# A spectral filter ahead of a GELU block: first and forward stage on sums and differences, forward stage in bursts of 64x64 tiles

## The chip, the cores and the metric

The kernel runs on one core of a Trainium2 chip. The metric is the device time of one launch in microseconds. Five engines work beside one another on that core: TensorE (PE in the profile, its weight loads PEld), VectorE (DVE), ScalarE (ACT), GpSimd (POOL) and SyncE (SP). POOL and SP issue most of the DMAs here.

## The reference

```python
X = np.fft.rfft(x, axis=1)                      # x: 8 x 3008 x 256
Y = X * (filt_r + 1j * filt_i)[None]            # 1505 frequencies x 256 channels
y = np.fft.irfft(Y, n=3008, axis=1)             # 8 x 3008 x 256
h = y.reshape(24064, 256) @ w_in                # 256 x 2048
g = 0.5 * h * (1 + erf(h / sqrt(2)))            # exact GELU
out = g @ w_out                                 # 2048 x 256, float32
```

## The kernel before

The transform of 3008 = 47 x 64 points is split: n = 64 n1 + n2, and k = k1 + 47 j. All arithmetic on TensorE takes bf16 or fp16 operands.

- **s1** is the first stage. It contracts over n1 (47) for each n2 and gives 24 values of k1 with a real and an imaginary part (48 rows). Each call of `s1(b, c)` does 16 of the 64 values of n2 in eight matmuls of 47x64 tiles with 512 columns, two tiles in the rows of the array by two in its columns. Four PSUM banks are evacuated (L306 on VectorE, L304 on ScalarE) and stored to R1 in DRAM by SP. `r1` reads R1 back with n2 and the real or imaginary part on the partitions.
- **s2** is the forward stage. For each k1 it contracts over n2 and re/im (128 rows) to 64 complex outputs (128 columns). One call `s2(b, p)` does two k1: two 128x128 matmuls of 256 columns (L427), and at once one VectorE product (L430) with the filter F, once for its real and once for its imaginary part.
- **s3** is the backward stage, four k1 pairs per call, sixteen 64x64 tiles with 512 columns (L444). Two `s3_out` evacuate to v_sb, stored to R2. `r2` reads it back as d_sb.
- **s4** finishes the inverse transform (L473) into the ring y_sb, 512 tokens of which form a token tile.
- **mm1** (L592) is y @ w_in for 128 hidden columns, followed by a GELU on ScalarE (L595). **mm2_seven** (L665) is g @ w_out in the seven products of Strassen's scheme: sums_1 (L634), sums_2 (L640) and sums_3 (L647) on VectorE make its operands, and VectorE adds its products (L680 to L694) from two PSUM banks ps_o into the output tiles ost, which POOL stores.

The order of all engines' work is written out by a list of slots. A token tile is 16 slots. A slot has one mm1 and seven matmuls of mm2_seven for the tile before (in the first 16 slots, mm1 alone). What else belongs to a slot is put into `at` by the function names, and issued ahead of the slot's mm2_seven and mm1. For each batch b from 1, `hi` is the slot at which its first token tile is due; s1, r1, s2 and s3 have fixed distances from it, s4 is placed backwards from its due slot into slots that are not in `busy`, and in `crowd` its evacuation goes to ScalarE. Batch 0 is transformed ahead of slot 0 by other functions (c1, c1t, c2, c3, c3t, c4), with its own tables.

PSUM has three banks "h" (mm1; also one bank of each s1 and s3), two "o" (ps_o) and three "f" (s1, s2, s3, s4). [...] `load_next` loads a part of the next batch of x from POOL, behind a `gate`: a one-element copy on POOL that waits for a product of s2. `load_filters_again` rewrites F from batch 0's layout to the one of the others.

Of the kernel before, what the change touches and what calls it, by code (L numbers as in the profile page):

```python
# [19 lines left out]
K1 = 24  # L20
# [11 lines left out]
class _Mix:  # L32
    def __init__(self, ctx, tc, x, filt_r, filt_i, w_in, w_out, out):
# [12 lines left out]
        self.pp = pool("pp", 6)  # L46
# [11 lines left out]
        self.T2p = c.tile([128, K1, 2, 2, 2, 16], BF16, name="T2p")  # L58
# [20 lines left out]
    def load_x(self, b, lo=0, n=32, hs=(0, 1)):  # L79
        nc = self.nc  # L80
        if lo == 0 and 0 in hs:
            self.st[b, "x"] = self.px.tile([128 if b else 2 * NA, HB, 256], BF16, tag="x", name="x_sb")
        xt, o = self.st[b, "x"], 64 if b else NA
        xv = self.x[b].rearrange("(n1 h w) d -> h n1 w d", h=2, w=HB)
        for w in range(lo, lo + n, 8):
            for h in hs:
                nc.gpsimd.dma_start(out=xt[h * o:h * o + NA, w:w + 8, :], in_=xv[h][:, w:w + 8, :])  # L87

# [20 lines left out]
    def load_filters_again(self, eng, k0, k):  # L109

        for o in range(0, 128, 32):
            i = self.st["Fd"][o // 64, :, :, :, k0:k0 + k, :].rearrange("q i t k c -> (q i) t (k c)")
            eng.dma_start(out=self.F[o:o + 32, :, k0:k0 + k, :], in_=i)
# [11 lines left out]
    def load_next(self, b, p, c, h):  # L125

        if b > 0:
            self.gate(self.st[b, "p", p][0:1, 0, 0:1])
        self.load_x(b + 1, 8 * c, 8, (h,))
# [41 lines left out]
    def table_2_rows(self, g):  # L171


        v = self.nc.vector
        ts = v.tensor_scalar
        col = lambda name, dt=FP32: g.tile([128, 1], dt, name=name)
        ri_i, h_i, w_i = col("ri_i", I32), col("h_i", I32), col("w_i", I32)
        ts(out=h_i, in0=self.pi, scalar1=1, scalar2=1, op0=ALU.logical_shift_right, op1=ALU.bitwise_and)
        ts(out=w_i, in0=self.pi, scalar1=2, scalar2=None, op0=ALU.logical_shift_right)
        ts(out=ri_i, in0=self.pi, scalar1=1, scalar2=None, op0=ALU.bitwise_and)  # L180
        self.n2, self.ri = col("n2"), col("ri")
        v.scalar_tensor_tensor(out=self.n2, in0=h_i, scalar=float(HB), in1=w_i, op0=ALU.mult, op1=ALU.add)
        ts(out=self.n2, in0=self.n2, scalar1=1.0 / self.S, scalar2=None, op0=ALU.mult)
        ts(out=self.ri, in0=ri_i, scalar1=-0.25, scalar2=TURNS + 0.25, op0=ALU.mult, op1=ALU.add)
# [40 lines left out]
    def weights_4(self, g):  # L225

        ts = self.nc.gpsimd.tensor_scalar
        h, q, self.wt, self.wts = (g.tile([128, 1], FP32, name=n) for n in ("h48", "q48", "wt", "wts"))
        ts(out=h, in0=self.p, scalar1=48.0, scalar2=None, op0=ALU.is_ge)
        ts(out=q, in0=h, scalar1=-48.0, scalar2=-1.0, op0=ALU.mult, op1=ALU.add)  # L230
        self.nc.gpsimd.tensor_tensor(out=q, in0=self.p, in1=q, op=ALU.add)
        self.nc.gpsimd.tensor_tensor(out=q, in0=q, in1=q, op=ALU.mult)
        ts(out=q, in0=q, scalar1=1.0, scalar2=-1.0, op0=ALU.is_equal, op1=ALU.mult)
# [43 lines left out]
    def table_3_copy(self, q, turn):  # L277

        k = slice(8 * q, 8 * q + 8)
        if turn < 2:  # L280
            self._evac(self.T3[:, k], self.t3.rearrange("p (k w e) -> p k e w", k=8, e=4), "act")
        if turn:
            v = self.t3.rearrange("p (k w h r) -> p k h r w", k=8, h=2, r=2)
            for r in range(2):
                self._evac(self.T3i[:, k, r::2, :], v[:, :, :, 1 - r, :], "act", self.turn[r])

    def table_3_turn(self, q):

        k = slice(8 * q, 8 * q + 8)
        for r in range(2):  # L290
            self.nc.vector.tensor_scalar(out=self.T3i[:, k, r::2, :], in0=self.T3[:, k, 1 - r::2, :],
# [27 lines left out]
    def table_2_parities(self):  # L319
        t = self.T2.rearrange("p k r (s j e) -> p k r s j e", s=2, e=2)  # L320
        for par in range(2):
            for q in range(2):
                self.nc.gpsimd.tensor_copy(out=self.T2p[:, :, par, :, q, :], in_=t[:, :, :, q, :, par ^ q])

    def table_u_rows(self, g):
# [3 lines left out]
        v.tensor_copy(out=self.u0[:, 0], in_=self.T3[:, 0, 0:2, :])  # L329
        v.tensor_copy(out=self.u0[:, 1], in_=self.T3i[:, 0, 0:2, :])  # L330
# [14 lines left out]
    def table_4_rows(self, g):  # L345
# [5 lines left out]
        for x in range(2):  # L351
            for r in range(2):
                t = self.T1[0:NA, 24 * (x ^ r):24 * (x ^ r) + 24].rearrange("p (a k) -> p a k", k=2)
                v.tensor_copy(out=self.T1g[:, x, r], in_=t.unsqueeze(2).to_broadcast([NA, 12, 2, 2]))
        t = self.T2.rearrange("p (a k) r j -> p r a j k", k=2)[:, 0, :, 0:2, :]
        for r in range(2):
            v.tensor_copy(out=self.T2g[:, r], in_=t)

    def table_4_factors(self, g):
# [7 lines left out]
        self.fcs = t[:, 96:224].rearrange("p (w h r) -> p w h r", h=2, r=2)  # L367
# [16 lines left out]
    def s1(self, b, c):  # L384
# [4 lines left out]
        if b == 1 and c == 3:  # L389
            a = [self.pp.tile([128, 2, 512], BF16, tag="p12", name="p12") for i in range(2)]  # L390
        else:
            at = self.pa.tile([128, 4, 512], BF16, tag="a", name="a_sb")
            a = [at[:, 0:2], at[:, 2:4]]
        x = self.st[b, "x"]
        ps = [[self.bank("ps_s1", "h" if i == h == 0 else "f") for h in range(2)] for i in range(2)]
        for i in range(2):
            for r in range(2):
                for h in range(2):
                    w = 8 * c + 4 * r + 2 * i
                    nc.tensor.matmul(ps[i][h][64 * r:64 * r + 64, :], lhsT=self.T1s[64 * h:64 * h + NA],  # L400
                                     rhs=x[64 * h:64 * h + NA, w:w + 2, :], start=True, stop=True)
        for i in range(2):
            for h in range(2):
                self._evac(a[i][:, :, 256 * h:256 * h + 256], ps[i][h].rearrange("p (w c) -> p w c", w=2),
                           "act" if h and (b > 1 or i) else False)
        o = self.st[b, "R1"].rearrange("(w h) q c -> q w h c", h=2)
        for r in range(2):
            w, q = 8 * c + 4 * r, slice(64 * r, 64 * r + 48)
            if b == 1 and c == 3:
                for i in range(2):  # L410
                    nc.sync.dma_start(out=o[:, w + 2 * i:w + 2 * i + 2], in_=a[i][q].rearrange("q w (h c) -> q w h c", h=2))
            else:
                nc.sync.dma_start(out=o[:, w:w + 4], in_=at[q].rearrange("q w (h c) -> q w h c", h=2))
# [8 lines left out]
    def s2(self, b, p):  # L422
        nc = self.nc
        ps = self.bank("ps_s2")
        for i in range(2):
            k = 2 * p + i
            nc.tensor.matmul(ps[:, 256 * i:256 * i + 256], lhsT=self.T2p[:, k].rearrange("p a b c d -> p (a b c d)"),  # L427
                             rhs=self.st[b, "b", k // 6][:, k % 6, :], start=True, stop=True)
        w = self.st[b, "p", p] = self.pp.tile([128, 2, 512], BF16, tag="p12", name="p12")
        nc.vector.tensor_tensor(out=w, in0=ps.unsqueeze(1).to_broadcast([128, 2, 512]),  # L430
                                in1=self.F[:, :, 2 * p:2 * p + 2, :].rearrange("p t a b -> p t (a b)"), op=ALU.mult)
# [18 lines left out]
    def s3_out(self, b, u, i):  # L450
        ps = self.st[b, "ps3"][i]
        vt = self.pv.tile([128, 4, 256], BF16, tag="v", name="v_sb")
        for par in range(2):
            self._evac(vt[:, 2 * par:2 * par + 2, :].rearrange("p a b -> p (a b)"), ps[par],
                       "act" if par or b < 3 else False)
# [30 lines left out]
    def c1(self, grp, half, eng):  # L486

        if grp == 0 and half == 0:
            n = 4 * K1 * 2 * HB
            self.at = self.y0[:, 4608:4608 + n].rearrange("c (a k n h r) -> c a k n h r", a=2, k=K1, h=2, r=2)  # L490
        ps = self.bank("ps_c1", "n")
        x = self.st[0, "x"]
        for i in range(4):
            self.nc.tensor.matmul(ps[:, 96 * i:96 * i + 96], lhsT=x[:, 4 * grp + i, 128 * half:128 * half + 128],
                                  rhs=self.T1c, start=True, stop=True)
        self._evac(self.at[:, half].rearrange("c k n h r -> c k n (h r)")[:, :, 4 * grp:4 * grp + 4, :],
                   ps[:, 0:384].rearrange("c (i k e) -> c k i e", i=4, e=4), eng)

    def c1t(self, q, eng):
# [3 lines left out]
        for i in range(8):  # L503
            self.nc.tensor.transpose(ps[:, 128 * i:128 * i + 128],
                                     self.at[:, i % 2, 4 * q + i // 2].rearrange("c n h r -> c (n h r)"), self.eye)
# [4 lines left out]
    def c2(self, p):  # L510

        nc = self.nc
        w = self.st[0, "p", p] = self.pp.tile([128, 2, 512], BF16, tag="p12", name="p12")
# [220 lines left out]
def kernel(  # L734
# [20 lines left out]
    m.load_x(0, 0, 8)  # L755
    m.k48 = m.iota(g, "k48", [128, 2, K1], [[0, 2], [1, K1]])
    m.load_x(0, 8, 8, (0,))
# [5 lines left out]
    m.load_x(0, 8, 8, (1,))  # L763
    cols = m.cols = m.iota(g, "cols", [128, 128], [[1, 128]])
    m.load_x(0, 16, 16)
# [11 lines left out]
    t3 = m.pg.tile([128, 2, K1, 4, HB], BF16, tag="g", name="T3")  # L777
# [10 lines left out]
    for u in range(16):  # L788
        m.c1(u // 2, u % 2, False if u in (1, 3, 5, 7, 8, 10, 12, 14) else act)
        if u == 3:  # L790
# [4 lines left out]
            nc.vector.tensor_copy(out=m.T1q, in_=m.T1.rearrange("p (h r k) -> p k h r", h=2, r=2))  # L795
# [47 lines left out]
    m.load_x(1)  # L843
# [23 lines left out]
    for b in range(1, B):  # L867
        hi = first(b)
        if b == 1:
            s1, n1, r1, s2, n2, group = 0, 3, 12, 28, 3, 14  # L870
        elif b == 2:
            s1, n1, r1, s2, n2, group = hi - 87, 3.7, hi - 73, hi - 64, 3.4, 14
        else:
            s1, n1, r1, s2, n2, group = hi - 94, 3.7, hi - 80, hi - 70, 3.4, 14
        unit = lambda p: s2 + group * (p // 4) + int(n2 * (p % 4))
        busy.update(range(s1 - 1, s1 + int(3 * n1) + 2))
        for c in range(4):
            put(s1 + int(c * n1), m.s1, b, c)
            put(r1 if c < 3 else unit(3) + 1, m.r1, b, c)
        for p in range(12):  # L880
            put(unit(p), m.s2, b, p)
            busy.add(unit(p))
            if p % 4 == 3:
                put(unit(p) + 3, m.s3, b, p // 4)
                put(unit(p) + 4, m.s3_out, b, p // 4, 1)
                busy.update(range(unit(p) + 2, unit(p) + 6))
        after[b] = unit(11) + 7
        crowd.update(range(s2, after[b]))
        if b + 1 < B:
            for i in range(8):  # L890
                put(unit(i + 2), m.load_next, b, i + 2, i // 2, i % 2)

    for b in range(1, B):
# [8 lines left out]
        for u in range(7, -1, -1):  # L902
            due = (b * S + GRP * u) // TCH * 16
            end = min(end, due - 2 + 6 * (u == 0 and b == 1))
            for half in (1, 0):
                while end in busy:
                    end -= 1
                assert end > after[b] + 8
                put(end, m.s4, b, u, half, act if half or end in crowd or b == 1 and u == 0 else False)
                busy.add(end)  # L910
                end -= 2
# [7 lines left out]
    put(3, m.table_4_factors, g)  # L919
    put(4, m.table_u)  # L920
# [58 lines left out]
```

## Time and profile before

| | |
|---|---|
| median of 3 runs | 746.34 us (745.94 to 746.36) |
| the profiled execution, its span | 747.16 us, 745.3 us |
| TensorE busy, matmuls | 728.5 us (98%), 8287 |
| VectorE busy, instructions | 573.2 us (77%), 1028 |
| ScalarE busy, instructions | 557.5 us (75%), 1000 |
| POOL busy, instructions | 227.7 us (31%), 424 |
| L430 products | 84 of 1220 ns |
| L427 forward matmuls | 168 |
| DMAs of x on POOL | 64 of 188 KB, 4.1 us to landing |

Busy time counts an instruction from its start to its end, and neighbours overlap: two matmuls of 512 columns start 0.22 us apart, though a record lasts 0.38 us. What an instruction costs its engine is the distance between starts, which the timeline view gives. A line with a count of xN is a run of N instructions of one kind.

### The profile page before, as it was taken

What the parts mean: (1) busy time and instruction counts of PE and PEld (TensorE: products, weight loads), DVE (VectorE), ACT (ScalarE), POOL (GpSimd) and SP (SyncE); (2) the same over time, 40 slices, a digit from 0 to 9 for tenths busy, and PEclk for the clock granted to TensorE, in tenths of its full rate; (3) what the DMA queues carried; (4) which work ended last, traced back from release to release, by engine and by line L of the source; (5) the groups of instructions that cost most, each with busy time, mean ns of one, the idle gap of its engine ahead of it and who ended that gap; (6) DMA issues with size and microseconds to landing.
All of it is one profiled execution on the core that took longest, in us unless ns stands there. A gap on an engine that the chain in (4) does not pass through costs nothing.

```text
span 745.3 us, 20244 instructions
## 1 busy us (share of the span) xinstructions
PE 728.5 (98%) x8287; PEld 518.7 (70%) x8420; DVE 573.2 (77%) x1028; ACT 557.5 (75%) x1000; POOL 227.7 (31%) x424
## 2 busy tenths in 40 slices
PE   7999999999999999999999999999999999999998
PEld 4856675766777776677777777677677766777776
DVE  7876877778678886789767996779957798676566
ACT  6996777777787777777777777877778777777773
POOL 7993216232312322133311342114311221112121
PEclk9999999999999999999999999999999999999999
DMA  8999743665266742657426654257533533401011
GB/s 140 218 234 244 141 97 102 190 113 132 68 162 154 141 98 72 171 143 133 122 64 172 135 112 123 71 157 145 125 100 94 145 111 92 117 29 58 30 58 58
DMA packets 76664, 90.74 MB, mean 122 GB/s; under 512 B 9755, under 2 KB 57883, under 8 KB 76315
## 3 DMA queue, kind: packets, MB, share of 16 engines
q1 hardware_dynamic: 58714, 49.63, 26.2%
q0 software_dynamic: 17440, 39.62, 24.2%
q8 instruction: 66, 1.08, 0.6%
q14 instruction: 28, 0.22, 0.1%
q10 hardware_dynamic: 416, 0.20, 0.1%
HBM read 57.15 MB, written 48.23 MB: 141 GB/s over the span
## 4 chain that ended last, share of the span: by engine, by line
PE 91%; DVE 2%; issue 2%; ACT 2%; DMA 2%; POOL 1%; DVEq 0%; POOLq 0%
PE ps_h L592 39%; PE ps_o L665 39%; PE ps_s L473 3%; PE ps_s L427 3%; PE ps_s L444 3%; PE ps_s L400 2%; ACT g_sb L595 1%; DMA x_sb<-in_x_dram 1%; PE ps_o L606 1%; DMA F<-in_filt_i_dram 1%; DVE p L521 1%; PE ps_c3t L554 1%; PE ps_c L539 0%; POOL x_sb L87 0%; DVE g_sb L640 0%
## 5 line engine op out<-in xcount | busy, mean ns | idle before, releaser
L595 ACT ACTIVATE g_sb<-ps_h 128x512 f16<-128x512 f32 x752 | 446.3, 600 | 166.8 <-PE ps_h L592 147.1
L592 PE MATMUL ps_h<-y_sb,w_in_sb 128*128 128x512 bf16 (+3 forms) x1471 | 417.5, 365 | 1.0
L665 PEld LDWEIGHTS <-g_sb 128*128 128x128 f16 x2944 | 194.8, 98 | 77.6 <-issue 12.8
L712 POOL DMA_DIRECT2D out_dram<-ost x221 | 125.0, 572 | 400.4 <-DVE ost L694 380.5
L665 PEld LDWEIGHTS <-s_sb 128*128 128x128 f16 x2208 | 148.7, 98 | 51.2 <-issue 5.8
L592 PEld LDWEIGHTS <-w_in_sb 128*128 128x128 bf16 x1600 | 125.0, 98 | 8.3 <-issue 1.7
L665 PE MATMUL ps_o<-w_sums,g_sb 128*128 128x128 f16 x1472 | 127.6, 219 | 2.0 <-DVE g_sb L640 0.9
L665 PE MATMUL ps_o<-w_sums,s_sb 128*128 128x128 f16 x1472 | 125.9, 219 | 0.9
L430 DVE TENSOR_TENSOR p<-ps_s,F 128x1024 bf16<-128x1024 f32 x84 | 102.4, 1220 | 26.8 <-PE ps_s L427 26.5
L634 DVE TENSOR_TENSOR s_sb<-g_sb 128x1024 f16<-128x1024 f16 x184 | 120.5, 683 | 1.0 <-ACT g_sb L595 1.0
L665 PE MATMUL ps_o<-w_out_sb,g_sb 128*128 128x128 f16 x1472 | 118.7, 219 | 0.9
L665 PE MATMUL ps_o<-w_out_sb,s_sb 128*128 128x128 f16 x736 | 63.8, 219 | 0.6
L640 DVE TENSOR_TENSOR g_sb<-s_sb,g_sb 128x1024 f16<-128x1024 f16 x92 | 63.1, 686 | 1.1
L647 DVE TENSOR_TENSOR s_sb<-g_sb 128x1024 f16<-128x1024 f16 x92 | 63.1, 686 | 0.0
L687 DVE TENSOR_TENSOR t_sb<-t_sb,ps_o 128x256 f32<-128x256 f32 x46 | 19.2, 418 | 46.5 <-PE ps_o L665 46.5
L473 PEld LDWEIGHTS <-d_sb 96*128 96x128 bf16 x448 | 31.9, 98 | 25.7
L306 DVE CAST a_sb<-ps_s 128x512 bf16<-128x512 f32 x57 | 36.6, 686 | 15.0 <-PE ps_s L400 14.9
L123 POOL COPY gate<-p 1x1 bf16<-1x1 bf16 x48 | 17.4, 363 | 96.8 <-DVE p L430 96.8
L682 DVE TENSOR_TENSOR ost<-t_sb,ps_o 128x256 f32<-128x256 f32 x46 | 19.2, 418 | 35.2 <-PE ps_o L665 35.0
L304 ACT ACTIVATE y_sb<-ps_s 128x376 bf16<-128x376 f32 x79 | 37.8, 479 | 2.6 <-PE ps_s L473 2.6
L473 PE MATMUL ps_s<-T4a,d_sb 96*128 96x94 bf16 x448 | 38.1, 206 | 1.1
L694 DVE TENSOR_TENSOR ost<-t_sb,ps_o 128x256 f32<-128x256 f32 x90 | 33.7, 415 | 6.6 <-PE ps_o L665 6.2
(149 smaller groups left out, 529.7 us busy)
## 6 DMA issues: line engine op xcount, KB each, us to landing
out_dram<-ost POOLq DMA_DIRECT2D x123, 128.0 KB, 2.2
x_sb<-in_x_dram POOLq DMA_DIRECT2D x64, 188.0 KB, 4.1
b_sb<-R SPq DMA_DIRECT2D x28, 384.0 KB, 4.1
R<-v_sb SPq DMA_DIRECT2D x84, 128.0 KB, 2.4
d_sb<-R SPq DMA_DIRECT2D x56, 192.0 KB, 4.5
R<-a_sb SPq DMA_DIRECT2D x54, 192.0 KB, 3.1
F<-Fd SPq DMA_DIRECT2D x4, 512.0 KB
Fd<-F SPq DMA_DIRECT2D x8, 192.0 KB, 7.2
```

Source lines behind the costliest of these rows:

```text
L304: self.nc.scalar.activation(out=out, in_=in_, func=AF.Copy, scale=1.0 if scale is None else scale)
L306: self.nc.vector.tensor_copy(out=out, in_=in_)
L430: nc.vector.tensor_tensor(out=w, in0=ps.unsqueeze(1).to_broadcast([128, 2, 512]), in1=self.F[:, :, 2 * p:2 * p + 2, :].rearrange("p t a b ...
L473: nc.tensor.matmul(ps[:, 94 * i:94 * i + 94], lhsT=d[:, (grp % 2) * 4 + i, 128 * half:128 * half + 128], rhs=self.T4a[:, 4 * grp + i], sta ...
L592: nc.tensor.matmul(ps[:, o:o + n], lhsT=w[:, dc], rhs=self.ring[:, dc, off:off + n], start=(dc == 0), stop=(dc == 1))
L595: nc.scalar.activation(out=self.st["g", t][:, jc, :], in_=ps, func=AF.Gelu)
L634: self.nc.vector.tensor_tensor(out=self.st["s", t][:, i:i + 2], in0=a, in1=b, op=ALU.subtract)
L640: self.nc.vector.tensor_tensor(out=a21[:, k], in0=self.st["s", t][:, k, 0], in1=a22[:, k], op=ALU.add)
L647: self.nc.vector.tensor_tensor(out=self.st["s4", t][:, k], in0=a12[:, k], in1=s2[:, k], op=ALU.subtract)
L665: nc.tensor.matmul(ps[:, (m + 1) % 2, sub, :], lhsT=a[:, i, 128 * sub:128 * sub + 128], rhs=b[:, i], start=i == 0, stop=i == 7)
L694: v(out=c(h, 1 - h), in0=tt, in1=p, op=ALU.add)
L712: eng.dma_start(out=out, in_=tile_[lo - r0:lo - r0 + n])
```

## The change

x(n) and x(n + 1504) have the same twiddle for an even frequency and opposite ones for an odd frequency. 1504 is 23.5 x 64, so x(n + 1504) is n1 + 23 (or + 24) in the other half of n2. The loads put the partner into the same partition, `fold` makes sum and difference on VectorE, s1 transforms both, and the forward stage then contracts over 32 values of n2 with re/im (64 rows) to 64 outputs, from the sums for the even and from the differences for the odd frequencies: a 64x64 tile each. Eight k1 form one burst of sixteen tiles with 256 columns, in four PSUM banks, followed by four products, one each second slot. Tables, filter layout and slots follow.

```diff
-        self.pp = pool("pp", 6)
+        self.pp = pool("pp", 3)                                  # tiles of twice the size
-        self.T2p = c.tile([128, K1, 2, 2, 2, 16], BF16, name="T2p")
+        self.T2p = c.tile([128, K1, 2, 2, 16], BF16, name="T2p")
+        self.xs = c.tile([128, 4, 256], BF16, name="xs")
...
+    def load_x_pairs(self, b, c, h, n=1):
+        xt = self.st["x1"]
+        xv = self.x[b].rearrange("(n1 h w) d -> h n1 w d", h=2, w=HB)
+        for v in range(2):
+            for to, at, m in ((0, 23, 24), (24, 0, 23)) if h else ((0, 0, NA),):
+                i = xv[h][at:at + m, 8 * c:8 * c + 8 * n].rearrange("m (a v w) d -> v m a (w d)", v=2, w=4)[v]
+                o = xt[64 * v + to:64 * v + to + m, h, 4 * c:4 * c + 4 * n].rearrange("p (a w) d -> p a (w d)", w=4)
+                self.nc.gpsimd.dma_start(out=o, in_=i)
+    def fold(self, b, c):
+        x, tt = self.st["x1"], self.nc.vector.tensor_tensor
+        k, n = slice(4 * c, 4 * c + 4), 64 + NA
+        s = self.st[b, "s", c] = x[:, 0, 4 * c - 4:4 * c] if c else self.xs
+        tt(out=s[0:n], in0=x[0:n, 0, k], in1=x[0:n, 1, k], op=ALU.add)
+        tt(out=x[0:n, 1, k], in0=x[0:n, 0, k], in1=x[0:n, 1, k], op=ALU.subtract)
...
     def load_filters_again(self, eng, k0, k):
-            eng.dma_start(out=self.F[o:o + 32, :, k0:k0 + k, :], in_=i)
+            if o < 64:
+                eng.dma_start(out=f.rearrange("p t k c -> p t (k c)"), in_=i.rearrange("p t k c -> p t (k c)"))
+            else:
+                for t in range(2):
+                    for e in range(2):
+                        eng.dma_start(out=f[:, t, e::2], in_=i[:, t, 1 - e::2])
...
     def s1(self, b, c):
+        x = self.st[b, "s", c], self.st["x1"][:, 1, 4 * c:4 * c + 4]
         for i in range(2):
+            for d in range(2):
+                for v in range(2):
+                    nc.tensor.matmul(ps[i][v][64 * d:64 * d + 64, :], lhsT=self.T1s[64 * v:64 * v + NA],
+                                     rhs=x[d][64 * v:64 * v + NA, 2 * i:2 * i + 2, :], start=True, stop=True)
-                           "act" if h and (b > 1 or i) else False)
+                self._evac(at[:, w:w + 2, :].rearrange("p w c -> p (w c)"), ps[i][v], "act" if v else False)
...
+    def s2(self, b, u):
+        self.st[b, "ps2"] = ps = [[self.bank("ps_s2", "h" if i == d == 0 else "f") for d in range(2)] for i in range(2)]
         for i in range(2):
+            for j in range(2):
+                for odd in range(2):
+                    for d in range(2):
+                        k, r = 8 * u + 4 * i + 2 * j + odd, slice(64 * d, 64 * d + 64)
+                        o = 64 * (odd ^ d)
+                        nc.tensor.matmul(ps[i][d][o:o + 64, 256 * j:256 * j + 256],
+                                         lhsT=self.T2p[r, k].rearrange("p a b c -> p (a b c)"),
+                                         rhs=self.st[b, "b", k // 6][r, k % 6, :], start=True, stop=True)
+    def s2_out(self, b, u, i, d):
+        if d == 0:
+            w = self.st[b, "w"] = self.pp.tile([128, 2, 4, 256], BF16, tag="p12", name="p12")
...
+        k = 8 * u + 4 * i + d
+        ps = self.st[b, "ps2"][i][d].rearrange("p (a c) -> p a c", a=2)
+        self.nc.vector.tensor_tensor(out=self.st[b, "w"][:, :, d:4:2, :], in0=ps.unsqueeze(1).to_broadcast([128, 2, 2, 256]),
+                                     in1=self.F[:, :, k:k + 3:2, :], op=ALU.mult)
...
     def s3_out(self, b, u, i):
-                       "act" if par or b < 3 else False)
+                       "act")
...
+        e = 4 * (b == B - 1)
+        s1, n1, r1 = (1, 4, 16) if b == 1 else (hi - 87, 3.7, hi - 73) if b == 2 else (hi - 94 - e, 3.7, hi - 80 - e)
+        s2 = (32, 46, 58) if b == 1 else (hi - 64 - 2 * e, hi - 48 - 3 * e, hi - 32 - 3 * e)
         for c in range(4):
+            put(slot - 1 if b == 1 else s1 - 28 + 6 * c, m.fold, b, c)
+            put(slot, m.s1, b, c)
+        for u in range(3):
+            put(s2[u], m.s2, b, u)
+            for i in range(4):
+                put(s2[u] + 2 * i, m.s2_out, b, u, i // 2, i % 2)
+            put(s2[u] + 10, m.s3, b, u)
+            put(s2[u] + 11, m.s3_out, b, u, 1)
+            busy.update(range(s2[u] - 1, s2[u] + 5), range(s2[u] + 9, s2[u] + 12))
+        after[b] = s2[2] + 15
+        crowd.update(range(s2[0], after[b]), range(s1 + 66, s1 + 94))
...
-                end -= 2
+                end -= 1 if u < 3 else 2
...
-    put(3, m.table_4_factors, g)
-    put(4, m.table_u)
+    put(8, m.table_4_factors, g)
+    put(9, m.table_u)
-    put(4, m.table_4_all, parts[:5])
-    put(80, m.table_4_all, parts[5:])
+    for i, slot in enumerate((10, 80, 96, 112)):
+        put(slot, m.table_4_all, parts[2 * i:2 * i + 2])
-    put(17, m.weight_sums)
+    put(19, m.weight_sums)
```

Before, s2 for batch b stood at hi - 70 + 14 (p // 4) + int(3.4 (p % 4)), with s3 three slots after each fourth (for batch 2, from hi - 64; for batch 1, from slot 28, three slots apart). In the tables, T2p is copied in 8 half-partition pieces for 4, and the tables of s3, s4 and batch 0 (T3, U, T4a, T2's rows) change their index order at the same sizes. Eight DMAs load x of batch 1 before; twelve do after.

## The prediction

> **What bounds the kernel now.** I read the engine shares and the chain of work that ended last first, then TensorE's timeline, then the two places where TensorE is not alone.
>
> ```profile
> span 745.3 us, 20244 instructions
> ...
> PE 728.5 (98%) x8287; PEld 518.7 (70%) x8420; DVE 573.2 (77%) x1028; ACT 557.5 (75%) x1000; POOL 227.7 (31%) x424
> ...
> PE 91%; DVE 2%; issue 2%; ACT 2%; DMA 2%; POOL 1%; DVEq 0%; POOLq 0%
> ```
>
> TensorE is the path. Its timeline (start, duration, engine, line) shows how full it is:
>
> ```profile
> 339.89 0.38 PE L427 MATMUL ps_s<-b_sb,T2p 128*128 128x256 bf16 x2
> 340.10 0.55 PE L665 MATMUL ps_o<-w_out_sb,g_sb 128*128 128x128 f16 x7
> 340.50 0.59 PE L592 MATMUL ps_h<-y_sb,w_in_sb 128*128 128x512 bf16 x2
> 340.93 0.55 PE L665 MATMUL ps_o<-w_out_sb,g_sb 128*128 128x128 f16 x7
> ...
> 342.14 0.38 PE L592 MATMUL ps_h<-y_sb,w_in_sb 128*128 128x512 bf16 x1
> 342.67 1.06 PE L444 MATMUL ps_s<-p,U 64*64 64x512 bf16 x16
> 343.65 0.56 PE L665 MATMUL ps_o<-w_sums,g_sb 128*128 128x128 f16 x7
> ```
>
> Starts, not durations, are the cost. One slot (seven L665, two L592) is 0.39 + 0.43 = 0.82 us. A pair of forward matmuls (L427) is 0.218 us: 0.109 each by their unrounded starts. The backward burst L444, sixteen 64x64 tiles with 512 columns, runs from 342.14 + 0.43 = 342.57 (one record of L592 is missing) to 343.65: 1.08 us. The first-stage burst L400, eight such tiles, takes 0.65:
>
> ```profile
> 300.71 0.59 PE L592 MATMUL ps_h<-y_sb,w_in_sb 128*128 128x512 bf16 x2
> 301.24 0.63 PE L400 MATMUL ps_s<-x_sb,T1s 47*64 47x512 bf16 x8
> 301.79 0.56 PE L665 MATMUL ps_o<-w_sums,s_sb 128*128 128x128 f16 x7
> ```
>
> So two more rows of four tiles cost 0.43 us, one row 0.215, and entering and leaving tiles 0.22.
>
> Two places differ. In the first 16 slots (39.35 to 49.83 us, s1 of batch 1 beside the first GELUs) the windows view has ScalarE busy 10.36 of 10.50 us. And VectorE can be late with the sums that L665 reads:
>
> ```profile
> 175.19 1.22 DVE L430 TENSOR_TENSOR p<-ps_s,F 128x1024 bf16<-128x1024 f32 x1
> 176.32 0.68 DVE L640 TENSOR_TENSOR g_sb<-s_sb,g_sb 128x1024 f16<-128x1024 f16 x1
> 177.06 0.51 PE L665 MATMUL ps_o<-w_sums,g_sb 128*128 128x128 f16 x6 [0.35 <-DVE g_sb L640]
> ```
>
> Successive VectorE starts: product 1.13, sum 0.60, output add 0.33 us.
>
> [...] the sixteen loads of L444 take 0.58 us in all, the second row's start 0.03 us after the first row's matmuls, in the same row groups, and the next row follows at 0.216.
>
> **The change part by part.**
>
> *Forward matmuls.* Removed: 12 pairs a batch, 12 x 0.218 = 2.62 us on the path. Added: 3 bursts of 16 tiles, four rows of 256 columns: 0.22 + 4 x 0.109 = 0.66, so 1.97. Gain 0.21 a burst, 21 bursts: **-4.4 us**. The loads are the unknown: they last 0.106 us, just under the 0.109 of a row. If hidden, -4.4; if a row waits for them, 0.215 a row, each burst 1.08, +4.4. I take hidden, as in L444.
>
> *fold.* 56 new tensor_tensors, at the nearest row's 683 ns (L634, starts 0.60 apart): 34 us of VectorE. In return 30 casts of v_sb (18 us) and 16 of 25 evacuations in s4 (8 us) move to ScalarE, as my listing of the slots from the loops shows. VectorE gains some 8 us of work, ScalarE 30 x 0.5 + 16 x 0.4 = 21; beyond slot 16 each stays under its slot on average. What hides them is their own idle time; what counts is where they stand in the queue.
>
> *The first 16 slots.* s1's right half always goes to ScalarE: 4 more evacuations at 0.5 us (starts of L304) on the busiest engine, +2.0. And fold(1,0) queues behind c4's last evacuations (end 39.84), takes two starts and a tail, 1.28 us; s1 in slot 1 waits for it until 41.1, when TensorE is free at 39.8. ScalarE then has one GELU to do and idles about 1 us. Less the 0.5 us that TensorE waits there already: **+2.4 us** (1.5 to 3.2). No later work of this stretch has slack, since TensorE is full from 49.8 on.
>
> *Products in bursts.* Same count and size (84 x 1220 ns[...]), but one every two slots where it was 3.4. Behind each on VectorE stand sums_2 and sums_1, for which L665 waits. Fifteen bursts (batches 2 to 6) begin at the head of a token tile. From the burst's start: product 0.53 to 1.66, sums_2 to 2.26, sums_1 to 2.86, product to 4.00, second sums_2 done at 4.68. TensorE wants it at 0.66 + 5 x 0.82 + 0.06, about 4.8. That just fits: 0, or up to 0.3 each (4.5 us). I take **+0.4** in all. The wait shown above (0.51 us, batch 2) goes, as its products move: **-0.5**.
>
> *Bursts at other places.* Batch 1's second burst (slot 46) puts products and the output adds ahead of sums_2: it ends at 7.1 us, wanted at 6.5: +0.65. Its third (slot 58) has fold(2,0) in the queue: the output adds that free a ps_o bank are done at 9.0, TensorE wants the bank at 7.4: +1.6. fold(7,0) (slot 530) stands between a product and sums_2 of a burst: 1.2 less the margin: +1.1. Batch 7's second burst follows a backward burst by two slots, and its "f" banks are evacuated 0.55 us late: +0.55. Together **+3.9** (1 to 5).
>
> *Loads and queues.* x needs 164 DMAs on POOL for 64, 100 x 0.53 = 53 us, and gates as before; POOL waits 380 us for output tiles, and its output DMAs stand ahead of the loads in each tile. Cover gone: a late ost buffer, seen twice before for 1.5 us in all. Folds come 14 or more slots (11 us) after their loads, which land in 4.1. On SP, s1's stores keep their number bar two, and the refill of F has 10 DMAs for 4, ready by slot 46; POOL's refill, 10 for 4 (5.5 us), and the table copies are due at slot 32, some 10 us after they end. T4a's parts are due 12 or more slots after theirs. All at nothing.
>
> **Sum.** -4.4 - 0.5 + 2.4 + 0.4 + 3.9 = +1.8. The profiled execution took 747.16 us (span 745.3, 1.9 around it), 0.8 above the median of 746.34. The difference is put on the median: 748.2 us.
>
> **The rivals.**
>
> *Faster.* The bursts gain their 4.4 and VectorE catches up before TensorE asks, since it runs ahead of its slots when nothing blocks it. For it: real VectorE waits of TensorE after 60 us are only three before. Against it: the sums above. It decides once the late-sum terms fall under 1 us: -4.9 + 2.4 + 0.5 = -2, 744.3; with half the ramp too, 743.1. Chance 0.23.
>
> *Even.* The terms are right but half of batch 1's and 7's waits hide in one another: -0.2, 746.1 to 747.5. Chance 0.29.
>
> *Forecast.* 747.9 to 750. Chance 0.34.
>
> *Head-of-tile bursts late.* [...] ScalarE's GELUs are late for sums_1: 0.3 at 15 bursts, 748.2 + 4.1 = 752.3. Chance 0.09.
>
> *Tiles not four at once.* The change would not do what it says: +8.8, 757. L444 speaks against it. Chance 0.05.
>
> **How the numbers follow.** 0.2% is 1.5 us, about what a measurement of this kernel can tell from no change. Slower 0.34 + 0.09 + 0.05 = 0.48, within 0.29, faster 0.23. The range 743.2 to 751.8 leaves out about 0.1 on either side.
>
> **What would show it.** Burst from the last L592 to the next L665: 0.66 us (1.08 would be the last rival). First L606 near 52.2 us for 49.83. L665 waiting for L640 or ps_o near batch 1's third burst. 84 products still near 1220 ns. If the first sixteen slots take under 11.5 us, or no L665 waits for VectorE by over 0.5 us, the forecast is wrong on the fast side.

## The result, and the profile after

The changed kernel takes **784.48 us** (784.37 to 786.07), the kernel before beside it 746.14 us: ratio 1.052, interval 1.0502 to 1.0538. That is 38 us slower, where 1.8 us were forecast. Lines of the page after:

```profile
span 784.2 us, 20767 instructions
...
PE 733.1 (93%) x8450; PEld 511.3 (65%) x8588; DVE 582.9 (74%) x1034; ACT 575.1 (73%) x1050; POOL 291.1 (37%) x540
...
PEclk9968999999999899999999999999999999999999
...
DMA packets 92249, 90.81 MB, mean 116 GB/s; under 512 B 20786, under 2 KB 70962, under 8 KB 92026
...
PE 76%; DMA 7%; ACT 5%; DVE 4%; issue 3%; POOL 3%; SPq 0%; DVEq 0%; POOLq 0%
...
L467 DVE TENSOR_TENSOR p<-ps_s,F 128x1024 bf16<-128x1024 f32 x84 | 102.5, 1220 | 6.5 <-PE ps_s L455 5.0
```

TensorE's busy time hardly grew, but its share of the chain fell from 91% to 76%, and DMA's rose from 2% to 7%: much of the time went into waiting for DMAs. The arithmetic itself came out as planned. There are 84 products of 1220 ns, the same mean as before. And a forward burst costs what was worked out (TensorE's timeline: start, duration, line):

```profile
278.66 0.38 PE L632 MATMUL ps_h<-y_sb,w_in_sb 128*128 128x512 bf16 x1
279.19 0.63 PE L455 MATMUL ps_s<-b_sb,T2p 64*64 64x256 bf16 x16
279.75 0.56 PE L705 MATMUL ps_o<-w_out_sb,g_sb 128*128 128x128 f16 x7
```

From 278.66 + 0.43 (one record of L632 is missing) to 279.75 it is 0.66 us.

To see where the 38 us lie, follow the GELUs, which come one a slot: the start of the k-th, after minus before, from the first one on.

| slots | what the change has there | after | e7 | e10 |
|---|---|---|---|---|
| 0 to 16 | batch 1's first stage | +23.8 | +3.7 | +1.9 |
| 16 to 64 | its forward bursts 1 to 3 | +0.8 | +0.8 | +1.3 |
| 64 to 128 | folds of batch 2, its first burst | +3.5 | +4.7 | +2.1 |
| 128 to 192 | the rest of batch 2 | -1.4 | -1.4 | -1.4 |
| 192 to 208 | s4 of batch 2 | **+7.4** | +0.1 | +0.1 |
| 208 to 288 | batch 3's bursts | -0.6 | -0.7 | -0.7 |
| 288 to 304 | s4 of batch 3 | **+6.1** | +0.1 | +0.1 |
| 304 to 528 | three more batches | -1.8 | -1.8 | -1.8 |
| 528 to 544 | fold(7,0) | +1.3 | +1.3 | 0.0 |
| 544 to the end | batch 7's bursts | +0.1 | +0.1 | -0.6 |
| sum | | +39.1 | +6.8 | +0.9 |

(e7 and e10 are experiments below. The profiled execution of before had its first GELU 1.6 us later than that of b1, whose kernel is the same up to there; so the table starts at the first GELU and its sums are about a microsecond above the differences of medians.)

Three places make 37 us of it. The waits view of after names them (us in all, times, longest):

```profile
PE ps_s L428 <- DVE xs L106: 14.0, 1, 14.0
DVE xs L106 <- DMA x_sb<-in_x_dram: 13.0, 1, 13.0
POOL x_sb L99 <- DMA x_sb<-in_x_dram: 10.1, 2, 9.2
...
PE ps_s L510 <- DMA d_sb<-R: 7.6, 3, 4.2
...
PE ps_s L428 <- DVE x_sb L106: 5.2, 1, 5.2
```

**Batch 1's x.** The view of the tile x_sb, limited to 28 to 60 us (ns min/median/max of one issue, then the landing), before and after:

```profile
L87 POOL DMA_DIRECT2D x_sb<-in_x_dram x8: 505/505/530, 30.6 to 34.1; - x8
...
DMA to landing us min/median/max: 3.7/6.3/8.2
```

```profile
L99 POOL DMA_DIRECT2D x_sb<-in_x_dram x12: 587/1097/1718, 29.4 to 51.8; - x12
...
DMA to landing us min/median/max: 7.9/16.5/18.7
```

The prediction had used 4.1 us, which is the median of all 64 old loads; batch 1's own took up to 8.2. The first fold starts at 51.6 us (at 39.2 in e7, where the loads are mended), and TensorE stands from 38.4 to 52.4. It stops a second time, for 5.2 us, until the fold of the third chunk has its last load, which lands at 63.8 us. After each stop TensorE runs at half rate for some microseconds: its granted clock is 0.50 from 52.4 to 55.7 us and again from 65.2 to 69.4, where before it is 1.00 throughout from 28 to 78 us.

**d_sb on SP.** SP's timeline before and after, then TensorE's after:

```profile
217.52 1.68 SPq L464 DMA_DIRECT2D d_sb<-R  x2
220.08 1.43 SPq L419 DMA_DIRECT2D b_sb<-R  x3
```

```profile
230.32 12.44 SPq L436 DMA_DIRECT2D R<-a_sb  x8
245.52 1.29 SPq L442 DMA_DIRECT2D b_sb<-R  x3
246.85 1.09 SPq L501 DMA_DIRECT2D d_sb<-R  x2
```

```profile
254.40 0.49 PE L510 MATMUL ps_s<-T4a,d_sb 96*128 96x94 bf16 x4 [4.23 <-DMA d_sb<-R]
254.69 0.95 PE L705 MATMUL ps_o<-w_sums,s_sb 128*128 128x128 f16 x7
255.43 1.06 PE L632 MATMUL ps_h<-y_sb,w_in_sb 128*128 128x512 bf16 x2
```

The r2 that fetches d_sb for s4 now stands behind three r1 of the next batch, which wait on SP until the stores R<-a_sb are done. Before, it stood ahead of them. Its data, too, come behind theirs: the three b_sb land 5.6 to 7.0 us after their issue, d_sb 7.0 after its own, for 3.7 before. The two matmuls of 512 columns after the stop last 1.06 us together, not 0.59: starts 0.427 us apart, not 0.216. The granted clock is 0.50 from 254 to 260 us and 1.00 from 261 to 264. Half rate lasted 3.3 us after the stop of 14 us, but about 6 us after this one of 4.2 us and after the next of 3.2 us (0.50 from 349.4 to 356.0 us). What sets its length is not shown.

### The profile page after: what moved, and what is told of

It reads as the page before. It is cut to its first block, busy times and chain, and to the rows that moved or that the text cites. A ratio compares the mean times of both kernels' runs of the same rounds, so it can differ in the third digit from the quotient of the medians.

```text
span 784.2 us, 20767 instructions
## 1 busy us (share of the span) xinstructions
PE 733.1 (93%) x8450; PEld 511.3 (65%) x8588; DVE 582.9 (74%) x1034; ACT 575.1 (73%) x1050; POOL 291.1 (37%) x540
## 2 busy tenths in 40 slices
DMA packets 92249, 90.81 MB, mean 116 GB/s; under 512 B 20786, under 2 KB 70962, under 8 KB 92026
## 3 DMA queue, kind: packets, MB, share of 16 engines
q0 software_dynamic: 31040, 39.66, 23.5%
## 4 chain that ended last, share of the span: by engine, by line
PE 76%; DMA 7%; ACT 5%; DVE 4%; issue 3%; POOL 3%; SPq 0%; DVEq 0%; POOLq 0%
PE ps_o L705 33%; PE ps_h L632 32%; DMA x_sb<-in_x_dram 4%; ACT g_sb L635 3%; PE ps_s L481 3%; PE ps_s L510 3%; DMA d_sb<-R 2%; PE ps_s L428 2%; PE ps_s L455 1%; ACT v_sb L329 1%; DVE s_sb L674 1%; DVE p L467 1%; DMA F<-in_filt_i_dram 1%; PE ps_o L646 1%; DVE g_sb L680 1%
## 5 line engine op out<-in xcount | busy, mean ns | idle before, releaser
L632 PE MATMUL ps_h<-y_sb,w_in_sb 128*128 128x512 bf16 (+3 forms) x1466 | 420.9, 369 | 0.7 <-ACT g_sb L635 0.2
L632 PEld LDWEIGHTS <-w_in_sb 128*128 128x128 bf16 x1600 | 126.1, 99 | 9.9 <-issue 4.7
L705 PE MATMUL ps_o<-w_sums,s_sb 128*128 128x128 f16 x1472 | 128.0, 221 | 1.8
L674 DVE TENSOR_TENSOR s_sb<-g_sb 128x1024 f16<-128x1024 f16 x184 | 120.1, 687 | 3.7 <-ACT g_sb L635 3.7
L467 DVE TENSOR_TENSOR p<-ps_s,F 128x1024 bf16<-128x1024 f32 x84 | 102.5, 1220 | 6.5 <-PE ps_s L455 5.0
L99 POOL DMA_DIRECT2D x_sb<-in_x_dram x156 | 86.3, 560 | 10.1 <-DMA x_sb<-in_x_dram 10.1
L687 DVE TENSOR_TENSOR s_sb<-g_sb 128x1024 f16<-128x1024 f16 x92 | 66.0, 717 | 0.0
L680 DVE TENSOR_TENSOR g_sb<-s_sb,g_sb 128x1024 f16<-128x1024 f16 x92 | 65.3, 710 | 0.7
L705 PE MATMUL ps_o<-w_out_sb,s_sb 128*128 128x128 f16 x736 | 63.8, 219 | 0.4
L329 ACT ACTIVATE y_sb<-ps_s 128x376 bf16<-128x376 f32 x95 | 47.2, 497 | 5.1 <-PE ps_s L510 5.1
L734 DVE TENSOR_TENSOR ost<-t_sb,ps_o 128x256 f32<-128x256 f32 x90 | 33.8, 417 | 22.7 <-PE ps_o L705 22.7
L331 DVE CAST a_sb<-ps_s 128x512 bf16<-128x512 f32 x54 | 34.8, 685 | 15.9 <-PE ps_s L428 15.6
L329 ACT ACTIVATE v_sb<-ps_s 128x512 bf16<-128x512 f32 x84 | 45.5, 597 | 0.2
```

Of the source, the lines that this page charges most:

```text
L99: self.nc.gpsimd.dma_start(out=o, in_=i)
L329: self.nc.scalar.activation(out=out, in_=in_, func=AF.Copy, scale=1.0 if scale is None else scale)
L331: self.nc.vector.tensor_copy(out=out, in_=in_)
L467: self.nc.vector.tensor_tensor(out=self.st[b, "w"][:, :, d:4:2, :], in0=ps.unsqueeze(1).to_broadcast([128, 2, 2, 256]), in1=self.F[:, :, k ...
L632: nc.tensor.matmul(ps[:, o:o + n], lhsT=w[:, dc], rhs=self.ring[:, dc, off:off + n], start=(dc == 0), stop=(dc == 1))
L674: self.nc.vector.tensor_tensor(out=self.st["s", t][:, i:i + 2], in0=a, in1=b, op=ALU.subtract)
```

## The experiments

Two theories stood at first. **A**: batch 1's loads are late because of their form, two runs of x per partition in one DMA. **B**: the d_sb waits come from the order on SP, because `end -= 1` for u < 3 moved r2 to the slot of r1. The rival of both was that the denser work (folds, bursts, more DMAs) is late as such and that neither edit would bring much.

### e1, e2, e3: each mended alone, and both

```diff
e1:
-    for c in (0, 2):
+    for c in range(4):
-            m.load_x_pairs(1, c, h, 2)
+            m.load_x_pairs(1, c, h)
e2:
-   put(after[b] if u == 0 else end - 8, m.r2, b, u // 2)
+   put(after[b] if u == 0 else min(end - 8, first(b + 1) - 83) if u == 2 and b > 1 else end - 8, m.r2, b, u // 2)
e3: both
```

> After, with batch 1's x loaded in 24 DMAs of one contiguous source run per partition (as the later batches are) instead of 12 DMAs of two runs. Theory A, the two-run form is what made the loads slow (7,722 packets of 4 bytes on POOL's queue between 28 and 52.9 us, landing 16.5 us): the loads land in 3 to 6 us, the first s1 starts near 42 us instead of 52.4, the 17th GELU (72.8 us after, 50.9 before) comes at 53 to 57 us, and the whole is 16 to 20 us shorter: 765 to 768. Rival, halving the packets of x to 2,048 bytes and tripling the DMAs is what costs: with 24 DMAs the first s1 is no earlier than 50 us and the whole stays within 5 us of 784.5.

> After, with the third readback of batches 2 and 3 (r2 for u = 2) put back to three slots before the readbacks r1 of the next batch, as the kernel before has it; on SP alone two DMAs change places with three. Theory A, SP's order is the cause: r2 stood behind three r1 that wait for R1's stores, so d_sb came 4.2 and 3.3 us late and TensorE ran at half its clock after each stop: the steps of +7.4 and +6.1 us at GELUs 208 and 304 vanish, 784.5 - 13.5 = 771. Rival, the readbacks are slow in themselves (x loads in smaller packets share the DMA engines): under 3 us are won.

> After, with both edits: one-run loads for batch 1, and r2 ahead of r1. Theory A (two separate faults outside the bursts): the gains add up, 784.5 - 18 - 13.5 = 753, and what is left against before (some +6) is the ramp's ScalarE and fold and batch 1's late sums. Rival, the bursts themselves cost: no more than 20 us are won, and the total stays over 764.

Measured: e1 764.81 us (ratio 1.0246, 1.0216 to 1.0275), e2 773.87 (1.0367, 1.0346 to 1.0388), e3 **754.31** (1.0106, 1.0086 to 1.0127). Against 784.48 these are -19.7, -10.6 and -30.2: the two faults add up. (For e2 13.5 were expected, and its trace has lost both steps, 13.4 us; but some 2 us more than in the trace of after lie ahead of slot 128, where nothing was changed. Why stays open.) In e1 24 DMAs carry the same bytes as 12 did, and land in 2.5 to 4.5 us:

```profile
L99 POOL DMA_DIRECT2D x_sb<-in_x_dram x24: 498/507/538, 29.5 to 41.7; - x24
...
DMA to landing us min/median/max: 2.5/3.5/4.5
```

In e2 both large steps at slots 192 and 288 shrink to 0.06 us. e3 left 8 us to explain.

### b1: the r2 order alone, in the kernel before

```diff
-   put(after[b] if u == 0 else end - 8, m.r2, b, u // 2)
+   put(after[b] if u == 0 else end - 5 if u == 2 and b in (2, 3) else end - 8, m.r2, b, u // 2)
```

> The kernel before, with only its third readback r2 of batches 2 and 3 put at the slot of the three r1, behind them on SP. Theory A: d_sb comes late there as well, two stops of 3 to 4.5 us with some slow matmuls after each, 746.1 + 9 to 14 = 755 to 760. Rival: within 3 us of 746.1.

Measured 763.46 us, ratio 1.0228 (1.0207 to 1.0248): +17.3 us, in two steps of 8.9 and nowhere else; 9 to 14 were expected, so the direction is shown and the size was set too low. So the order of two kinds of queue entries on SP is enough, without anything else of the change. Here the d_sb came still later than after the change (SP's timeline, then the waits):

```profile
218.52 2.39 SPq L419 DMA_DIRECT2D b_sb<-R  x3
220.96 1.98 SPq L464 DMA_DIRECT2D d_sb<-R  x4
```

```profile
PE ps_s L473 <- DMA d_sb<-R: 12.2, 2, 6.3
```

### e5, b2: what in the form of the loads

e5 is e2 with the two runs of each DMA sent to chunks c and c + 2, so that they lie apart in their destination too. This asks whether their neighbourhood matters (A1) or any two-run form does it (A2). The diff is condensed.

```diff
-                i = xv[h][at:at + m, 8 * c:8 * c + 8 * n].rearrange("m (a v w) d -> v m a (w d)", v=2, w=4)[v]
-                o = xt[64 * v + to:64 * v + to + m, h, 4 * c:4 * c + 4 * n].rearrange("p (a w) d -> p a (w d)", w=4)
+        xt = self.st["x1"].rearrange("p h (a c w) d -> p h c a (w d)", a=2, c=2)
+        xv = self.x[b].rearrange("(n1 h a c v w) d -> h c v n1 a (w d)", h=2, a=2, c=2, v=2, w=4)
+                dma_start(out=xt[64 * v + to:64 * v + to + m, h, c], in_=xv[h, c, v][at:at + m])
```

> e3_both, but batch 1's x in 12 DMAs of the sizes that the change has (188, 96 and 92 KB), each with two source runs, which now go to two separate places in a partition (chunks c and c + 2) instead of side by side. Theory A1, two runs that fall into one unbroken destination are what is split into 4-byte packets: fewer than 700 packets of 4 bytes on POOL's queue between 28 and 60 us, loads land in 3 to 7 us, and POOL is free 6 us sooner, so 749 to 752. Theory A2, any DMA with more than one source run per partition is: some 8,600 packets of 4 bytes again, and 765 to 772.

Measured 778.75 us (1.0437, 1.0416 to 1.0458), 4.9 more than e2, landing 7.8 to 18.9 us, and the trace's DMA records hold 8,620 packets of four bytes on POOL's queue between 28 and 60 us, exactly as many as after the change. A1 is out: the neighbourhood is not it.

b2 puts such loads into the kernel before. In it batch 1's rows of x change places, so its outputs for batch 1 are those of other rows; the bytes and the number of the loads stay.

```diff
-    m.load_x(1)
+    m.load_x_two_runs(1)     # 8 DMAs of 47 partitions; each takes the runs a = 0, 1 of
+                             # xv[h][:, w:w+16].rearrange("m (a v w) d -> v m a (w d)", v=2, w=4)[v]
```

> The kernel before, with batch 1's x loaded in 8 DMAs of 188 KB as before, but each with two source runs per partition that fall side by side into one destination run. Rows of x change places within batch 1, so batch 1's outputs are those of other rows; work and timing are otherwise the same. Theory A (the form alone): thousands of 4-byte packets, landing above 12 us, the first s1 or one of the next three late, 746.2 + 8 to 20 = 754 to 766. Rival (the form matters only with the change's other loads and queues): within 2 us of 746.2.

```profile
L98 POOL DMA_DIRECT2D x_sb<-in_x_dram x8: 1677/1692/1714, 29.7 to 41.3; - x8
...
DMA to landing us min/median/max: 18.3/19.7/21.4
```

766.02 us, ratio 1.0266 (1.0246 to 1.0287), +19.9 us, with 11,359 four-byte packets where the kernel before has 246. The form alone does it, in the kernel before too.

The separate issues of these runs gave the next lead. On POOL, a two-run load of 47 partitions takes 1.70 us and one of 23 takes 1.10; one of 24 takes 0.60. Loads of one run take 0.50 to 0.54 with 47, 24 and 23 alike (e1). A3 below, a guess from these times, puts the fault in two runs together with 47 or 23 partitions: with 48 and 24 it should go.

### e6, e7: one row more

```diff
-        xt = self.st["x1"]
-        xv = self.x[b].rearrange("(n1 h w) d -> h n1 w d", h=2, w=HB)
+        xt, r = self.st["x1"], b * self.S
+        xv = self.x.rearrange("b s d -> (b s) d")[r:r + 64 * (NA + n - 1)].rearrange("(n1 h w) d -> h n1 w d", h=2, w=HB)
-            for to, at, m in ((0, 23, 24), (24, 0, 23)) if h else ((0, 0, NA),):
+            for to, at, m in ((0, 23, 24), (24, 0, 22 + n)) if h else ((0, 0, NA + n - 1),):
e7: this, and r2 as in e2
```

> The changed kernel; batch 1's two-run loads take 48 partitions (or 24) each instead of 47 (or 24 and 23): one row more per piece, which lands on a partition that nothing reads; order, places and number of the loads stay. Theory A3: [...] the four-byte packets between 28 and 60 us fall from some 8,600 to under 1,000, the loads with 47 and 23 partitions issue in 0.6 us instead of 1.7 and 1.1, batch 1's x lands in 3 to 6 us, and the time is as with one-run loads or a little under it, 757 to 766 us. Theory A2 (any two-run form of these loads does it): 8,600 packets, landing 8 to 19 us, 782 to 787 us.

> The same, with r2 2.1 and r2 3.1 issued ahead of the next batch's three r1 on SP. Under A3 the twelve loads occupy POOL for some 7 us where the 24 one-run loads took 12.5, so the table work behind them starts some 5 us sooner, and the waits of TensorE for T2g and pick (1.0 and 2.3 us) and of ScalarE for wt (1.9 us) shrink or go: 749 to 754 us against 754.3 with 24 one-run loads and the same r2. If the tables are not what the first slots lose: 754 again. Under A2: 772 to 776 us.

Measured: e6 763.28 us (1.0234, 1.0218 to 1.0251), e7 **751.71** (1.0075, 1.0062 to 1.0088). e6's tile view:

```profile
L99 POOL DMA_DIRECT2D x_sb<-in_x_dram x12: 578/603/626, 28.8 to 35.2; - x12
...
DMA to landing us min/median/max: 3.7/5.8/7.3
```

Still 12 DMAs with two runs each, to the same places and one partition more; but 515 four-byte packets instead of 8,620, and 21.2 us less. So it is neither the two runs nor the number of DMAs, but **two runs with 47 or 23 partitions**. 48 and 24 are free of it. What sets these four counts apart is not shown, and no other was run with two runs. The small packets have a pattern: over the whole traces b2 has 11,272 more of four bytes than the kernel before, 1,409 for each of its eight loads, or about fifteen for each of a load's 94 runs; for a load of 23 partitions the same working (after against e6) gives 675, again about fifteen for each of its 46 runs. The count of partitions alone is not the reason: loads of one run with 47 and 23 land in 2.5 to 4.5 us (e1). What the small packets are, and why the two-run form makes them, stays open.

### e4: the tables later

e3, with the table work moved out of the first 16 slots.

```diff
-    put(8, m.table_4_factors, g)
-    put(9, m.table_u)
-    for i, slot in enumerate((10, 80, 96, 112)):
+    put(18, m.table_u)
+    put(26, m.table_4_factors, g)
+    for i, slot in enumerate((27, 80, 96, 112)):
```

> Both edits of the run before (one-run loads, r2 ahead of r1), and table_u moved from slot 9 to 18, table_4_factors from 8 to 26, the first table_4_all from 10 to 27. In e3_both TensorE waits 1.0 us for T2g and 2.3 us for pick, and ScalarE 1.9 us for wt, all from POOL, which has 24 load DMAs ahead of them. Theory A: these waits go, the first 16 slots end some 4.5 us sooner (17th GELU at 51.8 to 52.8 us instead of 56.3), the whole at 749 to 750.5. Rival: the first slots are bound by fold and ScalarE at the same place, and less than 2 us is won.

Measured 752.35 us (1.0078, 1.0061 to 1.0095), 2.0 below e3 (the two intervals overlap), where 749 to 750.5 were expected. The first 16 slots ended 3.1 us sooner, since TensorE no longer waits for T2g (1.0 us) and pick (2.3) nor ScalarE for wt (1.9). But 2.3 us came back in the slots after them, in a new wait:

```profile
51.91 0.60 PE L646 MATMUL ps_o<-w_out_sb,g_sb 128*128 128x256 f16 x4 [0.77 <-DMA w_out_sb<-in_moe_w_out_dram]
...
55.53 0.60 PE L646 MATMUL ps_o<-w_out_sb,g_sb 128*128 128x256 f16 x4 [1.67 <-DMA w_out_sb<-in_moe_w_out_dram]
```

POOL issues w_out behind the 24 loads of x, at some 43 us. With 12 clean loads it issues it at 36.8 us (e7), and e7 has neither wait.

### e8, e9, e10: what is left, slot by slot

e7's remaining stops had addresses, so the slots were moved.

```diff
e8 (against e7):
-        s1, n1, r1 = (1, 4, 16) if b == 1 else ...
+        s1, n1, r1 = (3, 4, 20) if b == 1 else ...
-            put(slot - 1 if b == 1 else s1 - 28 + 6 * c, m.fold, b, c)
+            put((0, 5, 9, 13)[c] if b == 1 else (70, 73, 83, 86)[c] if b == 2 else s1 - 28 + e + 6 * c, m.fold, b, c)
     (tables as in e4; r2 1.1 at slot 93; batch 7's second burst two slots later)
e9 (against e8): r1 at 17, SP's load of F from 17 to 18, batch 2's folds at 68, 70, 73, 75
+   "act" if v and (b, c) != (1, 3) else False        # s1's last chunk of batch 1 evicted by VectorE alone
e10 (against e9): folds of batch 1 at 0, 2, 6, 10, of batch 2 at 54, 68, 71, 91
```

> e7 (48-row loads, r2 ahead) with its slots moved where its TensorE still stops for something the change brought: batch 1's first stage at slots 3, 7, 11, 15 instead of 1, 5, 9, 13 with r1 at 20 and the table work at 18, 26, 27, so that ScalarE has fewer evictions in the first 16 slots (they cost 3.7 us there); batch 2's folds at 70, 73, 83, 86 instead of 61, 67, 73, 79, out of VectorE's crowded slots (stops of 1.8 and some 1.0 us); r2 1.1 at 93 instead of 100 (0.9); batch 7's folds four slots later (1.3 in e7), and its second burst two slots later (f banks). Theory: what is left of the loss in e7, 5.4 us, is these stops, and the bursts give 0.6 us a batch: 743 to 748 us. Rival: the burst form costs the early slots this much wherever the folds lie, the stops move to the next wait: 750 to 753.

Measured **755.34** us (1.0129, 1.0111 to 1.0147): slower than e7, a miss. Two of the moves ran into something. SP's timeline, and TensorE's:

```profile
54.68 8.56 SPq L139 DMA_DIRECT2D F<-Fd  x8
64.12 1.61 SPq L442 DMA_DIRECT2D b_sb<-R  x3
```

```profile
69.79 0.52 PE L455 MATMUL ps_s<-b_sb,T2p 64*64 64x256 bf16 x12 [4.27 <-DMA b_sb<-R]
```

r1, put at 20, had fallen behind the ten loads of F on SP that stand at slot 17 (the last eight are shown): fault B once more, with other names. And a fold met POOL (VectorE's timeline, then POOL's):

```profile
121.48 2.65 DVE L106 TENSOR_TENSOR x_sb<-x_sb 111x1024 bf16<-111x1024 bf16 x1
124.17 1.35 DVE L107 TENSOR_TENSOR x_sb<-x_sb 111x1024 bf16<-111x1024 bf16 x1
```

```profile
121.96 1.62 POOL L410 TENSOR_TENSOR tmp_sb<-t_sb 96x376 f32<-96x376 f32 x2
123.65 1.32 POOL L412 TENSOR_TENSOR T4a<-tmp_sb 96x376 bf16<-96x376 f32 x1
```

The fold took 2.65 and 1.35 us for its usual 0.68 and 0.69, and each of its two halves ended 0.55 us after an instruction of POOL did. By the profile the first half starts ahead of POOL's (121.48 against 121.96) and was held all the same. What holds it is not shown; that it was POOL is read from these times alone.

It was not the only case. In e7, whose folds lie elsewhere, sums_2 meets the same POOL lines in slot 116, and TensorE stops for it (VectorE's timeline, then TensorE's):

```profile
150.73 2.08 DVE L680 TENSOR_TENSOR g_sb<-s_sb,g_sb 128x1024 f16<-128x1024 f16 x1
```

```profile
152.87 0.51 PE L705 MATMUL ps_o<-w_sums,g_sb 128*128 128x128 f16 x6 [1.08 <-DVE g_sb L680]
```

POOL's lines L410 and L412 run from 150.63 to 153.65 us there. In e10 the same sum takes 2.07 us and TensorE stops 0.97: this stop is left in the best version. The change itself had spread this table work over the slots 80, 96 and 112.

> e8 with its two new stops taken out. (1) r1 goes to slot 17, ahead of the ten F loads on SP, which go to 18: in e8 r1 stood behind them (8.6 us on SP), b_sb came 4.4 us late and TensorE ran at half rate after it, 6.5 us together. (2) batch 2's folds go to 68, 70, 73, 75, away from POOL's work on T4a: the one at slot 86 took 2.65 us beside it instead of 0.69, and TensorE stopped for 1.9. (3) The last of batch 1's four first-stage chunks is evicted by VectorE alone, 1.1 us less for ScalarE in the first 16 slots. Theory: each stop is its own mistake of place, nothing is owed to the burst form: 755.3 - 6.3 - 1.9 - 1.1, so 744.5 to 747.5 us. Rival: VectorE has no room for all folds in batch 1's stages, and the stop only moves to another slot: 748 to 752.

> e9 with two groups of folds placed by VectorE's free time. Batch 1's folds at slots 0, 2, 6, 10, each one ahead of the evictions of the chunk before, so that TensorE's three stops for a fold in the first 16 slots (0.3 to 0.6 us each) go: the slots end 0.5 to 0.9 us sooner. Batch 2's at 54, 68, 71, 91, since VectorE idled 2.4 us at slot 55 and had work without a gap from 66 to 80, where TensorE stopped for 1.0 us: that one goes. Theory (VectorE's room in single slots is what is left): 747.7 - 0.7 - 1.0, so 745 to 747 us, equal to the kernel before. Rival (the first 16 slots are bound by the sum of VectorE's and ScalarE's work, and the fold at 91 stops TensorE in turn): 747 to 749.

Measured: e9 747.67 us, ratio 1.0020 (1.0012 to 1.0028); e10 **746.10**, ratio 0.9996 (0.9987 to 1.0004). e10 is inside what its theory said, e9 just above its own (744.5 to 747.5), and one part of e9 failed: VectorE alone on the last chunk did not shorten the first 16 slots (+2.8 in e8 and e9), and TensorE's waits for folds there were 0.7 us in e9. Putting the folds ahead (e10) gave 0.9 us.

So the 38 us divide by the runs: loads 21.2 (784.48 to e6), r2 order 11.6 (e6 to e7), slots and tables 5.6 (e7 to e10), and what is left is no difference. The first two were each changed alone; the 5.6 are many moves together, of which only some were read singly. No version measured here beats the kernel before.

## Why the prediction was right or wrong

- **Forward matmuls, -4.4 us: right.** A burst is 0.66 us (19 of the 21 in the trace after run like the one shown; the two others wait for "f" banks), and loads of the next row are hidden. A steady batch gains 0.60 to 0.65 us, three bursts at 0.21. The wait of 0.51 us of batch 2 is gone too: TensorE has no such stop between slots 128 and 192.
- **fold hidden: right in the steady batches** (in e7 TensorE has no stop over 0.25 us in slots 208 to 528), on the argument of VectorE's own idle time. It is not so where a slot's queue is full, and the forecast named two of those places.
- **Bursts at other places, +3.9: right within some 0.2 us each, where they can be read singly.** Slot 46 was put at +0.65, and TensorE stops 0.68 there; slot 58 at +1.6, measured 1.8; fold(7,0) at +1.1, measured 1.3; batch 7's "f" banks at +0.55, measured 0.69, and 0.6 came back when e8 moved that burst. (The -1.4 at slots 624 to 640, inside the last row of the table, is in e8 and e10 as well: work of batch 7 that now stands ahead of slot 624.) One was not named: the "f" banks of batch 1's third burst, 0.69 too.
- **Products at the head of a tile, +0.4: a little high.** The steady batches show the full gain of the bursts, so it was nothing.
- **First 16 slots, +2.4: the terms were right, but not all.** e7, with landing mended, has +3.7, e10 +1.9. In e7 the folds stop TensorE twice more there (0.29 and 0.21 us) and a GELU once (0.43), which was not in the sum.
- **"Loads and queues ... All at nothing": the step that failed.** Three things in it, and a smaller one. First, "which land in 4.1" is the landing of the old form, taken over for a DMA of two runs and 47 or 23 partitions that no trace of before showed; it was 7.9 to 18.7, worth 21.2 us. And the "14 or more slots" between load and fold hold for the later batches only: batch 1's first load is issued some 10 us ahead of its first fold. A form not yet seen needed a bound on its dear side. Second, the paragraph counted the DMAs on SP and not their order: `end -= 1` is quoted in the diff, and it moves r2 to the slot of the next batch's r1, which stands in the same diff. That was 11.6 us. Third, POOL's table work "due ... some 10 us after" its end was checked for slot 32 only, not for T2g, wt and pick in the first 16 slots behind the new loads: 5.2 us of waits of two engines in e3, of which e4 won 3.1 in those slots and lost 2.3 again behind them. "T4a's parts" were put at nothing by their due slots alone, but a sum of VectorE beside POOL's work on them took 2.08 us for 0.68 (1.08 us of TensorE in e7).
- **The sum, +1.8.** (746.34 and 1.8 give 748.1 rather than 748.2; nothing hangs on it.) With the first two mended, e7 is +5.4, at 751.71 just inside the range; the 3.6 us between lie in the first 16 slots (+3.7 for 2.4) and in slots 64 to 128 (+4.7, where the named stop is 1.6). Of the stops there that were not named, e7's trace shows 0.73 us for d_sb in slot 108 and the 1.08 beside POOL in slot 116.
- **The rivals.** None had this cause. "Tiles not four at once" came nearest in size and is excluded by the burst above. "Faster" let VectorE catch up before TensorE asks. In the first 128 slots it did not: even e10 loses 5.3 us there, and gains 4.4 later. That no placing could win them back is not shown.

## What to carry to other kernels

When a change gives a DMA a new shape, take no landing time from the old one: look for the same count of partitions and runs in a trace, and where a count is dear, as 47 in two runs was here (1.70 us to issue for 0.60), try 48, even if a row more is loaded for it: here that won 21.2 us. When a slot moves, write out each DMA queue around it in its order and ask what the entry ahead is waiting for; e8 shows how easily it happens twice. When tables are made on POOL beside a busy VectorE, look which sums they meet: here one of 0.68 us took 2.08. And a stop of TensorE of some microseconds cost more here than its length, since the granted clock was 0.50 for some 6 us afterwards: stops of 4.2 and 3.2 us made steps of 7.4 and 6.1.

## What the runs showed of the hardware that was not expected

- A DMA issued by POOL with two runs per partition: 1.70 us to issue and 18 to 21 us to land with 47 partitions (b2), 0.60 and 3.7 to 7.3 with 48 and 24 (e6), in spite of more bytes, and 0.50 to 0.54 and 2.5 to 4.5 with 47, 24 and 23 partitions in one run (e1). The page shows it as "under 512 B": 20,786 packets after, 12,450 in e6 and e10.
- A VectorE tensor_tensor of two SBUF operands took 2.65 us (e8), 2.08 (e7) and 2.07 (e10) for 0.68 beside POOL's tensor_tensors; those of e8 and e7 ended 0.55 us after one of POOL's.
- After stops of 3.2, 4.2 and 14 us TensorE's 512-column matmuls start 0.427 us apart for 0.216, at a granted clock of 0.50 for 1.00.
- A DMA of d_sb issued right behind three larger ones on SP lands 7.0 and 6.3 us after its issue (after, batches 2 and 3), for 3.7 and 4.3 (before) and 5.1 (e2, batch 2) ahead of them.
